# Attention by feature: sums over tokens turned, scores in row halves of the array, two heads gathered by DMA, and a new order of the first region

## The chip, the cores and the metric

One core of a Trainium2 chip. Its engines run side by side, each through its own list of instructions in order: TensorE (PE; its weight loads are shown apart as PEld), VectorE (DVE), ScalarE (ACT), GpSimd (POOL) and SyncE (SP), on whose queue all DMAs of this kernel are issued. The metric is the device time in microseconds (us), median of several runs; lower is better.

## What is computed

A gated linear attention with complex decays (4 batches, 8 heads, 768 tokens, 48 features a head), then a soft mixture of experts over all 3072 tokens, then a mixture with one expert a token. Cut to what matters here, the attention:

```python
mag = np.sqrt(a_re * a_re + a_im * a_im)
scale = np.minimum(mag, 0.999) / (mag + 1e-06)
for t in range(S):
    new_re = ar * S_re - ai * S_im        # ar, ai: a_re * scale, a_im * scale at t, by feature d
    new_im = ar * S_im + ai * S_re
    S_re, S_im = (new_re + kv, new_im)    # kv[d, e] = k[t, d] * v[t, e]
    y[:, :, t] = np.einsum('bhd,bhde->bhe', q[:, :, t], S_re)
x = attn_out.transpose(0, 2, 1, 3).reshape(B * S, H * D)
x = _moe_ref(x=x, **moe_kwargs)           # softmax over tokens, 8 experts x 4 slots, 384 -> 1024 -> 384
return _moe2_ref(x=x, **moe2_kwargs)      # one expert a token
```

## The kernel before

The tokens are worked on in 24 units of 128 tokens: 4 batches of 6 chunks. The program has three regions, one after the other, each with its instructions declared to a small scheduler (`Sched`) and then issued in an order written out by hand (`ORDER`, one string a region): a list of 16-bit numbers, each 4 x the number of the instruction + the variant, which says on which of two engines an instruction with a choice runs. The first region holds attention and the running softmax over tokens and ends with the slot inputs `siT`; the second holds the slot experts; the third the one expert a token and the output. The change is in the first.

In the first region, `decl_A` takes the decays of a group of one or two units (768 columns: 2 units x 384 features) through logarithms and an arctangent. `decl_B` makes, for a unit, the sums over its tokens of log decays and of phases: a product of a triangle of ones (`tri`) with a [128 tokens x 384 features] tile, result by token (`cumsum`, line 422 on). For most units it runs as two products in a shorter float format, of a high part (line 432 or 433) and a low part (434 or 435). The last token's sum is carried into the first row of the next unit's tile (lines 453 and 464, one partition of 384 columns), so a unit's sums start from those of the unit before; the first unit of a batch gets a start value (448). Then come the exponentials (455, 457), k and q times these (458, 459), rounding of the phases (466, 467) and, for a group, sine and cosine (475, 476).

`decl_C` multiplies k and q by cosine and sine into `kqp` (493; two instructions of 768 columns a unit, on VectorE or GpSimd), by token. Sixteen transposes a unit (503) turn it into 112-row tiles `kT`, `qT` (cosine part in rows 0 to 47, sine part in 64 to 111), which are copied from PSUM (helper `copy`, line 386, on ScalarE or VectorE). Scores of a head are one product of 112 rows (513), masked by VectorE (519). The output of a pair of heads comes from masked scores times v (526) and state times q (530), two heads side by side in the column halves of the array; the products of k and v (538) go the same way and are added to the state (559). The output is copied (`yT`), turned (569) and copied again (`x`). `decl_M` makes the running softmax over tokens for four units at a time.

The weights of the experts come on the same queue: eight arrays `wr` (1.5 MB each) during the first region, five arrays `wl` (line 364 too) that take the place of tiles of the first region as these become free, and the last three arrays in six halves (765) in the place of the first ones. The slot experts' first layer is line 748, the second 777.

Of the kernel before, what the change touches and what calls it, by code (L numbers as in the profile page):

```python
# [1355 lines left out]
```

## Time and profile before

| | |
|---|---|
| time, median of 3 runs | 331.19 us (330.14 to 333.09) |
| span of the profiled execution | 333.4 us |
| TensorE busy, whole span | 292.8 us (88%) |
| VectorE busy | 271.5 us (81%) |
| ScalarE busy | 223.9 us (67%) |
| GpSimd busy | 102.0 us (31%) |
| DMA moved | 57.98 MB |

Busy time is a share of the whole span; the regions have different limits, so the section of rows further down gives it by stretch. A row of the groups by line reads: line, engine, operation, written tile <- read tiles, shapes, count | busy time in us, mean duration in ns | idle time of the engine just ahead of these, and what ended it. Line 386 is a helper, there the tile tells. A float32 product has two records in the trace.

### The profile page before, as it was taken

What the parts mean: (1) busy time and instruction counts of PE and PEld (TensorE: products, weight loads), DVE (VectorE), ACT (ScalarE), POOL (GpSimd) and SP (SyncE); (2) the same over time, 40 slices, a digit from 0 to 9 for tenths busy, and PEclk for the clock granted to TensorE, in tenths of its full rate; (3) what the DMA queues carried; (4) which work ended last, traced back from release to release, by engine and by line L of the source; (5) the groups of instructions that cost most, each with busy time, mean ns of one, the idle gap of its engine ahead of it and who ended that gap; (6) DMA issues with size and microseconds to landing.
All of it is one profiled execution on the core that took longest, in us unless ns stands there. A gap on an engine that the chain in (4) does not pass through costs nothing. (4 is left out here: it accounts for less than half of the span.)

```text
span 333.4 us, 7852 instructions
## 1 busy us (share of the span) xinstructions
PE 292.8 (88%) x3152; PEld 230.4 (69%) x3152; DVE 271.5 (81%) x520; ACT 223.9 (67%) x417; POOL 102.0 (31%) x66
## 2 busy tenths in 40 slices
PE   0998989899886999998898969998999999999990
PEld 0676776778655779776587857887888433689880
DVE  3799999999999999999999998998555832557750
ACT  4999788689767889887878893887342321434670
POOL 0023456344515357533273553434400000000000
PEclk9999999979999999999979989999999999965996
DMA  7976887486574234235212320325693495290492
GB/s 231 298 317 241 308 312 262 170 312 229 168 243 152 77 80 159 73 105 180 73 49 73 101 81 12 94 73 191 201 361 77 132 375 186 47 334 1 154 328 96
DMA packets 27709, 57.98 MB, mean 174 GB/s; under 512 B 1824, under 2 KB 17568, under 8 KB 27664
## 3 DMA queue, kind: packets, MB, share of 16 engines
q1 hardware_dynamic: 27664, 57.39, 51.3%
q8 instruction: 27, 0.44, 0.5%
q14 instruction: 18, 0.15, 0.1%
HBM read 52.66 MB, written 4.72 MB: 172 GB/s over the span
## 5 line engine op out<-in xcount | busy, mean ns | idle before, releaser
L493 POOL TENSOR_TENSOR kqp<-kqi,lt 128x768 f32<-128x768 f32 x31 | 63.9, 2069 | 68.2 <-ACT lt L475 17.9
L503 PE MATMUL bank<-cst,kqp 128*112 128x128 f32 x384 | 54.3, 278 | 3.1 <-DVE lt L467 1.8
L513 PE MATMUL bank<-qT,kT 112*128 112x128 f32 x384 | 54.8, 289 | 1.9 <-DVE qT L386 1.8
L513 PEld LDWEIGHTS bank<-qT,kT 112*128 112x128 f32 x384 | 48.8, 198 | 6.8 <-DVE qT L386 2.4
L503 PEld LDWEIGHTS bank<-cst,kqp 128*112 128x112 f32 x384 | 41.9, 134 | 11.4 <-issue 6.5
L526 PE MATMUL bank<-sc,v 128*48 128x128 f32 x384 | 37.0, 279 | 3.8 <-DVE sc L519 2.0
L684 ACT ACT_TABLE_LOAD x29 | 37.2, 1283 | 1.2 <-PEq L1339 0.8
L519 DVE TENSOR_TENSOR sc<-bank,cst 128x512 f32<-128x512 f32 x48 | 32.5, 685 | 3.4 <-PE bank L513 2.8
L530 PE MATMUL bank<-qT,St 112*48 112x128 f32 x320 | 31.3, 272 | 0.0
L406 POOL TENSOR_TENSOR lt<-reim,lt 128x768 f32<-128x768 f32 (+1 forms) x11 | 19.4, 1760 | 34.9 <-ACT lt L405 34.3
L435 POOL TENSOR_TENSOR hl<-lt,hl 128x384 fp32r<-128x384 f32 x15 | 17.6, 1176 | 34.9 <-ACT hl L433 31.7
L526 PEld LDWEIGHTS bank<-sc,v 128*48 128x48 f32 x384 | 19.9, 122 | 10.1 <-issue 2.8
L538 PEld LDWEIGHTS bank<-v,kqp 128*48 128x48 f32 x640 | 18.0, 129 | 9.1 <-issue 4.0
L538 PE MATMUL bank<-v,kqp 128*48 128x48 f32 x640 | 22.2, 217 | 1.8 <-DVE St L559 1.3
L433 ACT ACTIVATE hl<-lt 128x384 fp32r<-128x384 f32 x28 | 14.5, 520 | 12.9 <-DVE lt L453 9.3
L439 PE MATMUL bank<-hl,trir 128*128 128x384 f32 x34 | 14.9, 437 | 5.8 <-DVE kqi L458 3.0
L1008 POOL TENSOR_TENSOR Pm<-G,pos 128x128 fp32r<-128x128 f32 x1 | 0.6, 644 | 63.0 <-DVE G L1003 63.0
L493 DVE TENSOR_TENSOR kqp<-kqi,lt 128x768 f32<-128x768 f32 x17 | 19.0, 1125 | 0.7 <-PE bank L538 0.7
L386 ACT COPY kT<-bank 112x512 f32<-112x512 f32 x28 | 16.3, 584 | 4.8 <-PE bank L503 4.8
L530 PEld LDWEIGHTS bank<-qT,St 112*48 112x48 f32 x320 | 19.3, 123 | 0.0
L682 PE MATMUL bank<-cst 128*48 128x128 f32 x78 | 11.0, 301 | 8.0 <-DMA cst<-cst 8.0
L386 DVE COPY qT<-bank 112x512 f32<-112x512 f32 x23 | 15.6, 683 | 2.4 <-PE bank L503 2.2
(248 smaller groups left out, 651.8 us busy)
## 6 DMA issues: line engine op xcount, KB each, us to landing
wr<-w SPq DMA_DIRECT2D x8, 1536.0 KB, 8.8
kqi<-kq SPq DMA_DIRECT2D x24, 384.0 KB, 3.4
reim<-reim SPq DMA_DIRECT2D x11, 768.0 KB, 5.5
wl<-w SPq DMA_DIRECT2D x5, 1536.0 KB, 7.2
v<-v SPq DMA_DIRECT2D x24, 192.0 KB, 2.4
wr<-w SPq DMA_DIRECT2D x6, 768.0 KB, 9.1
out<-osb SPq DMA_DIRECT2D x10, 384.0 KB, 2.6
wl<-m2w SPq DMA_DIRECT2D x2, 768.0 KB, 5.2
```

The costliest lines, as they stand in the source:

```text
L386: v = {"A": ("ACT", t_act(n, True), lambda: nc.scalar.copy(out=out, in_=in_()), False), "D": ("DVE", t_dve(n), lambda: vec.tensor_copy(out ...
L406: either("P", n, lambda e: e.tensor_tensor(out=l1, in0=im, in1=l0, op=ALU.mult), r=[kim] + k0, w=k1)
L435: e.tensor_tensor(out=hl[:, 1], in0=src, in1=hl[:, 0].bitcast(F32), op=ALU.subtract))
L439: pe.matmul(o(), trir, hl[:, 0], start=True, stop=False)
L493: either(e, 768, lambda e, dst=dst, j=j: e.tensor_tensor(out=dst, in0=kq, in1=b(j), op=ALU.mult), r=src + [kj], w=[kd])
L503: pe.transpose(bank(kb)[:112, 128 * i:128 * i + 128], o[:, j, 4 * hf + i], idn)
L513: pe.matmul(bank(kb)[:, 128 * i:128 * i + 128], kTt[ik[hf]][:, i], qTt[iq[hf]][:, i], start=True, stop=True)
L519: op("DVE", t_dve(512), lambda: vec.tensor_tensor(out=sct[ic[hf]], in0=b4(), in1=msk, op=ALU.mult), r=[kb], w=[ksc])
L526: pe.matmul(yps[64 * i:64 * i + 48, pr], v[:, 48 * h:48 * h + 48], sct[ic[hf]][:, h - 4 * hf], start=True, stop=(c == 0))
L530: pe.matmul(yps[64 * i:64 * i + 48, pr], St[:, h], qTt[iq[hf]][:, h - 4 * hf], start=False, stop=True)
L538: pe.matmul(kvps[64 * i:64 * i + 48, h, :48], o[:, 0, h, 64 * i:64 * i + 48], v[:, 48 * h:48 * h + 48], start=True, stop=True)
L684: tab = lambda t: nc.scalar.preload_act_table_set(TABLES[t])
```

## The change

All in the first region, with what hangs on it:

- k, q and the decays lie **by feature**: the host packs a unit's 384 features as three groups of 128, each with two heads of 48 in rows 0 to 47 and 64 to 111; heads 6 and 7 are cut in pieces of 16 rows that lie in rows 48 to 63 and 112 to 127 of the three groups (`feature_rows`).
- The sums over tokens are **turned**: the tile of decays is the stationary side, the triangle the moving one, three products of 128 columns, and the result is by feature. All are float32; high and low parts are gone, and so is the carry: sums start anew in each chunk. Phases get the last column of the unit before added (`pct`), and the state is multiplied by the chunk's whole decay (`Dt`) after each chunk.
- Products with cosine and sine go into `F` (by feature, so no turning is needed for the scores). The pieces of heads 6 and 7 are **gathered** from `F` into `M` by six DMAs a unit, 16 rows each.
- k alone is turned, for the products with v (six transposes in 20 units). Scores are products of 48 rows, cosine part and sine part added up, two heads at a time in the **row halves** of the array, each into a bank of its own. Products with the state use quarters of the array.
- Numbers of buffers change (k, q: 3 to 2), the first region has seven banks to pick from and one for k times v (before six, and one each for k times v and y), the scheduler knows the array's shapes (`MODE`), and the first region's order is a new string; so where DMAs, weights too, stand in SP's list is new.

By the new string, of 24 or 48 each: products F: 35 on VectorE, 13 on GpSimd; remainders of phases (20): 5 and 15; state products (20, four of them on VectorE only): 6 and 14; copies of turned k, 288 columns (40): 34 ScalarE, 6 VectorE; 96 columns (40): 29 and 11; copies of yT (48): 39 and 9; of x: 18 and 6; small copies of one or three columns: 27 ScalarE, 26 VectorE, 31 GpSimd. The arrays of `wr` go out in the order 3, 2, 0, 7, 5, 4, 6, 1; the array 4 ahead of the last unit's gathers, 6 and 1 after them, at the end of the list.

```diff
+XC = (0, 1, 0, 1)
+def pair(q):
+    return (2 * q + XC[q], 2 * q + 1 - XC[q])
+def feature_rows():
+    f = np.zeros((3, 128), np.int64)
+    for j in range(3):
+        for i in range(2):
+            f[j, 64 * i:64 * i + 48] = 48 * pair(j)[i] + np.arange(48)
+            f[j, 64 * i + 48:64 * i + 64] = 48 * pair(3)[i] + 16 * j + np.arange(16)
+    return f.reshape(-1)
-NR, NL, NK, NV, NKQ, NY, NX, NT, NTK, NTQ, NWR = 2, 3, 3, 4, 2, 4, 4, 2, 2, 3, 8
+NR, NL, NK, NV, NF, NKT, NSC, NY, NX, NWR = 2, 3, 2, 4, 2, 2, 4, 5, 5, 8
...
+MODE = [[0 if i == j else 95 if j else 24 for j in range(5)] for i in range(5)]
...
+            if e == "PE":
+                t0 = max(t0, free.get(e, 0.0) + MODE[mode][self.modes[i]])
...
@@ decl_B @@
+            def f():
+                for i in range(3):
+                    pe.matmul(bank(kb)[:, 128 * i:128 * i + 128], lt[:, j, 128 * i:128 * i + 128], (tri, tri2)[j], start=True, stop=True)
+            op("PE", 655, f, r=[kin, "cst"], w=[kb], acq=kb)
...
-            op("DVE", t_dve(384), lambda: vec.tensor_tensor(out=ln1, in0=oL()[96:97], in1=ln1, op=ALU.add), r=[kL, kn1], w=[kn1])
...
+        copy("D", 3, Dt[:, u, :3], lambda: oL3()[:, :, 127], r=[kL], w=[("D", u, 0)])
+        if c < NC - 1:
+            either("P", 3, lambda e: e.tensor_copy(out=Ft[u % NF][:, :, 512:513], in_=Dt[:, u, :3, None]), r=[("D", u, 0)], w=[("F", u % NF, 2)])
...
+            op("DVE", t_dve(384), lambda: vec.tensor_tensor(out=l3[1], in0=oP3(), in1=pct[(u - 1) % 2][:, :, None].to_broadcast([128, 3, 128]), op=ALU.add), r=[kP, ("pc", (u - 1) % 2)], w=[kth])
+            op("DVE", t_dve(384, True), lambda: vec.tensor_scalar(out=n, in0=lt[:, 1], scalar1=MAGIC, scalar2=MAGIC, op0=ALU.add, op1=ALU.subtract), two=True, r=[kth], w=[kn])
+            either("P", 384, lambda e: e.tensor_tensor(out=lt[:, 1], in0=lt[:, 1], in1=n, op=ALU.subtract), r=[kth, kn], w=[kth])
+        if c < NC - 1:
+            last = l3[1][:, :, 127]
+            op("DVE", 70, lambda: vec.tensor_copy(out=pct[u % 2], in_=last), r=[kth], w=[("pc", u % 2)], alt=(("ACT", 96, lambda: nc.scalar.copy(out=pct[u % 2], in_=last), False),))
@@ decl_C @@
-        Tr(0, 0, "A")
...
+        for i, e in ((0, "P"), (1, "D")):
+            b = lt[:, i].rearrange("p (j t) -> p j t", j=3)[:, None].to_broadcast([128, 2, 3, 128])
+            either(e, 768, lambda e, i=i, b=b: e.tensor_tensor(out=Fv[:, i], in0=kq, in1=b, op=ALU.mult), r=[(kkq, 0), (kkq, 1), klt(u, i)], w=[kF[i]])
+        for i in range(2):
+            for j in range(3):
+                d, o = 64 * i + 16 * j, 64 * i + 48
+                dma(32768, lambda j=j, d=d, o=o: nc.sync.dma_start(out=M[d:d + 16, :nx], in_=F[o:o + 16, j, :nx]), r=kF + kX, w=[("M", u % NF, i, j)])
+        if kX:
+            either("P", 1, lambda e: e.tensor_copy(out=Dt[:112, u, 3:], in_=M[:112, 512:513]), r=kM, w=[("D", u, 1)])
+        def kind(q, i, x):
+            t = F[64 * i:64 * i + 48, q] if q < 3 else M[64 * i:64 * i + 48]
+            return t[:, 128 * x:128 * x + 128]
...
+                        pe.transpose(bank(kb)[:, 128 * j:128 * j + 128], F[:, j, 128 * x:128 * x + 128], idn)
...
+                copy("A", 288, kTt[b][:, :288].rearrange("p (j i r) -> p j i r", j=3, i=2), lambda kv4=kv4: kv4()[:, :, :, :48], r=[kb], w=[("kT", b, 0)])
+                copy("D", 96, kTt[b][:, 288:].rearrange("p (i j r) -> p j i r", j=3, i=2), lambda kv4=kv4: kv4()[:, :, :, 48:], r=[kb], w=[("kT", b, 1)])
...
+                for q in qs:
+                    for x in range(2):
+                        for i in range(2):
+                            pe.matmul(bank(kbs[i])[:, 128 * q:128 * q + 128], kind(q, i, x), kind(q, i, 2 + x), start=(x == 0), stop=(x == 1))
...
+        op("PE", 870, SC((0, 1)), r=kF, w=kbs, acq=kbs[1], mode=2)
+        op("PE", 870, SC((2, 3)), r=kF + kM, w=kbs, mode=2)
...
+        def out(q, i, m):
+            o = 64 * (i ^ XC[q])
+            return bank(kby[XC[q]])[o:o + m, 128 * (q // 2):128 * (q // 2) + 128]
...
+                        pe.matmul(out(q, i, 64), v[:, 48 * h:48 * h + 64], sct[scs[i]][:, q], start=True, stop=(c == 0))
...
+                for x in range(2):
+                    for q in qs:
                         for i in range(2):
+                            pe.matmul(out(q, i, 48), S[64 * i:64 * i + 48, q, 48 * x:48 * x + 48], kind(q, i, 2 + x), start=False, stop=(x == 1))
...
+                op("DVE", t_dve(384), lambda: vec.tensor_tensor(out=Ut, in0=kvv, in1=S, op=ALU.add), r=[("kv", 0), ("kv", 1), kS], w=["U"])
+                either("P", 384, lambda e: e.tensor_tensor(out=S1, in0=Ut, in1=dcy, op=ALU.mult), r=["U"] + kD, w=[kS1])
...
+            copy("A", 256, yT[:, i::2], lambda i=i: bank(kby[i])[:112, :256].rearrange("p (q t) -> p q t", q=2), r=[kby[i]], w=[(kyT, i)])
...
-    s.emit(tab, fill(6), 600, 400, kv_last[0], kv_first[0], WARM)
+    s.emit(tab, fill(7), 600, 400, kv_last[0], kv_first[0], WARM)
```

## Rows read from the trace of the kernel before

**Rows 1.** The page: its first line.

```profile
span 333.4 us, 7852 instructions
```

**Rows 2.** The chain of waits, around and behind the end of the first region: start, length, what.

```profile
260.90 0.25 ACT siT L386
...
279.62 5.30 PE bank L777 x64
```

**Rows 3.** Busy time by stretch: stretch, length, each engine, granted clock, DMA share, GB/s.

```profile
0.00:20.00 20.00, 11.62 (x54) 7.98 (x54) 12.07 (x23) 14.56 (x22) 2.02 (x9) 1.00 0.88 290
20.00:200.00 180.00, 160.16 (x1874) 130.67 (x1874) 176.37 (x306) 150.50 (x269) 82.69 (x48) 0.98 0.50 166
200.00:236.00 36.00, 33.60 (x414) 28.53 (x414) 31.58 (x60) 24.56 (x50) 14.16 (x8) 0.98 0.28 87
236.00:261.20 25.20, 24.55 (x318) 20.56 (x315) 15.48 (x37) 8.89 (x24) 2.46 (x1) 1.00 0.76 249
```

**Rows 4.** Groups of instructions by line, VectorE.

```profile
L453 DVE TENSOR_TENSOR lt<-bank,lt 1x384 f32<-1x384 f32 x20 | 11.2, 558 | 1.0 <-ACT bank L455 0.5
...
L434 DVE SCALAR_TENSOR_TENSOR hl<-lt,hl 128x384 fp32r<-128x384 f32 x18 | 13.8, 769 | 0.0
...
L432 DVE TENSOR_SCALAR hl<-lt 128x384 fp32r<-128x384 f32 x6 | 2.1, 353 | 0.0
...
L386 DVE COPY qT<-bank 112x512 f32<-112x512 f32 x23 | 15.6, 683 | 2.4 <-PE bank L503 2.2
...
L493 DVE TENSOR_TENSOR kqp<-kqi,lt 128x768 f32<-128x768 f32 x17 | 19.0, 1125 | 0.7 <-PE bank L538 0.7
...
L466 DVE TENSOR_SCALAR n<-bank 128x384 bf16<-128x384 f32 x24 | 13.1, 551 | 0.2
```

**Rows 5.** Groups of instructions by line, ScalarE.

```profile
L386 ACT COPY kT<-bank 112x512 f32<-112x512 f32 x28 | 16.3, 584 | 4.8 <-PE bank L503 4.8
...
L433 ACT ACTIVATE hl<-lt 128x384 fp32r<-128x384 f32 x28 | 14.5, 520 | 12.9 <-DVE lt L453 9.3 <-DVE lt L464 3.6
...
L386 ACT COPY x<-bank 128x384 f32<-128x384 f32 x13 | 6.2, 475 | 0.8 <-PE bank L569 0.7
```

**Rows 6.** Groups of instructions by line, GpSimd.

```profile
L493 POOL TENSOR_TENSOR kqp<-kqi,lt 128x768 f32<-128x768 f32 x31 | 63.9, 2069 | 68.2 <-ACT lt L475 17.9 <-ACT lt L476 14.6 <-PE bank L538 9.5
...
L435 POOL TENSOR_TENSOR hl<-lt,hl 128x384 fp32r<-128x384 f32 x15 | 17.6, 1176 | 34.9 <-ACT hl L433 31.7 <-PE bank L616 3.2
```

**Rows 7.** Products: the chain of waits, then the timeline (start, length, engine, line).

```profile
238.29 0.88 PE bank L503 x8
...
239.52 0.22 PE bank L530 x4
...
241.64 0.89 PE bank L513 x8
...
229.68 0.45 PE L439 MATMUL bank<-hl,trir 128*128 128x384 f32 x1
...
229.97 0.34 PE L440 MATMUL bank<-hl,trir 128*128 128x384 f32 x1
```

**Rows 8.** DMA issues (count, KB each, median us to landing); the queue of SP.

```profile
v<-v SPq DMA_DIRECT2D x24, 192.0 KB, 2.4
...
wr<-w SPq DMA_DIRECT2D x8, 1536.0 KB, 8.8
...
3.13 2.15 SPq L423 DMA_DIRECT2D v<-v  x4
```

**Rows 9.** The queue of SP, the last product kqp, and stretches with weights under way.

```profile
224.96 30.29 SPq L364 DMA_DIRECT2D wl<-w  x5
...
237.46 2.46 POOL L493 TENSOR_TENSOR kqp<-kqi,lt 128x768 f32<-128x768 f32 x1 [2.97 <-ACT qT L386]
...
236.00:248.00 12.00, 12.00 (x173) 10.16 (x173) 6.87 (x10) 3.35 (x6) 2.46 (x1) 1.00 0.97 324
...
271.00:279.00 8.00, 8.00 (x89) 2.83 (x81) 3.29 (x9) 0.00 (x0) 0.00 (x0) 1.00 1.06 371
```

More of the change, by code (lines that the diff above doesn't have):

```diff
@@ L141, in place @@
         fb = [(0.0, b) for b in range(self.nbanks)]
-        order, end, port, cur, held = [], 0.0, 0.0, self.tab, {}
+        order, end, port, cur, held, mode = [], 0.0, 0.0, self.tab, {}, 0
         heap = [(key[i], i) for i in range(n) if nd[i] == 0]
@@ L250, in put @@
         c[:, o:o + w] = a
-    tri = (PERM[:, None] <= PERM[None, :]).astype(np.float32)
+    tri = np.triu(np.ones((128, 128), np.float32))
     put("tri", tri)
@@ L419, in decl_B @@
         lt = lt_of(u)
+        l3 = [lt[:, j].rearrange("p (j t) -> p j t", j=3) for j in range(2)]
         kln, kth = klt(u, 0), klt(u, 1)
@@ L508, in SC @@
-        def SC(hf):
-            kb = s.bank()
-            def f():
-                for i in range(4):
-                    pe.matmul(bank(kb)[:, 128 * i:128 * i + 128], kTt[ik[hf]][:, i], qTt[iq[hf]][:, i], start=True, stop=True)
-            op("PE", 870, f, r=[("kT", ik[hf]), ("qT", iq[hf])], w=[kb, ("sc", ic[hf])], acq=kb)
-            msk = tri[:, None].to_broadcast([128, 4, 128])
-            b4 = lambda: bank(kb).rearrange("p (h t) -> p h t", h=4)
-            ksc = ("sc", ic[hf])
-            op("DVE", t_dve(512), lambda: vec.tensor_tensor(out=sct[ic[hf]], in0=b4(), in1=msk, op=ALU.mult), r=[kb], w=[ksc])
@@ new lines, in decl_C, with SC @@
+        kbs = [s.bank() for _ in range(2)]
+        scs = [(2 * u + i) % NSC for i in range(2)]
+        def SC(qs):
+            def f():
+                for q in qs:
+                    for x in range(2):
+                        for i in range(2):
+                            pe.matmul(bank(kbs[i])[:, 128 * q:128 * q + 128], kind(q, i, x), kind(q, i, 2 + x), start=(x == 0), stop=(x == 1))
+            return f
+        op("PE", 2, lambda: None, r=kF, w=[kbs[0]], acq=kbs[0], mode=2)
+        op("PE", 870, SC((0, 1)), r=kF, w=kbs, acq=kbs[1], mode=2)
@@ new lines, in decl_C, with f @@
+        op("PE", 870, SC((2, 3)), r=kF + kM, w=kbs, mode=2)
+        for i in range(2):
+            msk = tri[:, None].to_broadcast([128, 4, 128])
+            op("DVE", t_dve(512), lambda i=i, msk=msk: vec.tensor_tensor(out=sct[scs[i]], in0=bank(kbs[i]).rearrange("p (h t) -> p h t", h=4), in1=msk, op=ALU.mult), r=[kbs[i]], w=[("sc", scs[i])])
+        if c < NC - 1:
+            for x in range(2):
+                t, kt = kTs[x]
+                def f(x=x, t=t):
+                    for q in range(4):
+                        for i in range(2):
+                            w = t[:, 96 * q + 48 * i:96 * q + 48 * i + 48]
+                            h = pair(q)[i]
+                            pe.matmul(kvps[64 * i:64 * i + 48, q, 48 * x:48 * x + 48], w, v[:, 48 * h:48 * h + 48], start=True, stop=True)
+                kv_first.append(len(s.ops))
+                op("PE", 472, f, r=kt + [kv] + ([("kv", 0)] if x else []), w=[("kv", x)], mode=1)
@@ new lines, in decl_C, with intra @@
+        kby = [s.bank() for _ in range(2)]
+        kS = ("S", (u - 1) % 2)
+        S = St[(u - 1) % 2]
+        def out(q, i, m):
+            o = 64 * (i ^ XC[q])
+            return bank(kby[XC[q]])[o:o + m, 128 * (q // 2):128 * (q // 2) + 128]
+        def intra(qs):
+            def f():
+                for q in qs:
+                    for i in range(2):
+                        h = pair(q)[i]
+                        pe.matmul(out(q, i, 64), v[:, 48 * h:48 * h + 64], sct[scs[i]][:, q], start=True, stop=(c == 0))
+            return f
@@ L562, in decl_C @@
         yT, kyT = yTt[u % NY], ("yT", u % NY)
-        copy("A", 512, yT, lambda: yps[:112], r=[("y", 0), ("y", 1)], w=[kyT])
+        for i in range(2):
+            copy("A", 256, yT[:, i::2], lambda i=i: bank(kby[i])[:112, :256].rearrange("p (q t) -> p q t", q=2), r=[kby[i]], w=[(kyT, i)])
         kb = s.bank()
@@ L1167, in build @@
             nc.sync.dma_start(out=p96, in_=a["phi96"])
[L1168 removed]
             def load_x(u):
                 b0, t0 = ORD[u][0] * 4 * D, ORD[u][1] * 128
[L1172 to L1174 removed]
+                for i in range(2):
+                    nc.sync.dma_start(out=xu[:, :, i], in_=ysc[t0:t0 + 128, i, b0:b0 + 4 * D].rearrange("t (q e) -> t q e", e=D))
             for u in range(NU):
@@ L1316, in layout @@
     return {
-        "reim": pack("a_re", "a_im"),
-        "kq": pack("k", "q"),
+        "reim": np.ascontiguousarray(pack("a_re", "a_im")[..., rows]),
+        "kq": by_feature("k", "q"),
         "v": pack("v").reshape(NU, 128, DM),
@@ L1353, in unpack @@
     for u, (b, c) in enumerate(ORD):
-        out[b, c, PERM] = o[u]
+        out[b, c] = o[u]
     return out.reshape(B * S, DM)
```

278 lines of the change are left out of this document (120 added, 158 removed).

## The prediction

> **What bounds the kernel now.** I read the busy time by stretch first, then the chain of waits at the end, then the groups of instructions by line. All sums are made on the profiled execution, whose span is 333.4 us [rows 1]; the median of the three timed runs is 331.19, so the last step takes 2.2 us off. The first region (attention and the running softmax over tokens) ends when siT is written, at 261.2; the rest takes 72.2 us [rows 1, 2]. In the long middle of that region, 20 to 200 us, VectorE works 176.4 of 180 us, 98%; TensorE has 160 there, ScalarE 150, GpSimd 83 [rows 3]. So what ends last in the middle is the queue of VectorE. Only in the last 25 us before siT is TensorE the fuller one, 24.55 of 25.2 (97%), with VectorE at 15.5 [rows 3]. Over the first region VectorE sums to 12.1 + 176.4 + 31.6 + 15.5 = 235.5 us, TensorE to 229.9, ScalarE to 198.5, GpSimd to 101.3 [rows 3].
>
> **The change part by part.** The order table is a list of numbers, each 4 x instruction + variant. Read against the declarations it says which engine takes each instruction, and in which order; for the kernel before these counts are those of the trace (18 low parts and 17 products kqp on VectorE, 28 high parts on ScalarE) [rows 4, 5], so I use them for the new one.
>
> *VectorE, removed.* The carries from one unit into the first row of the next: 20 + 20 at 0.558 us though they touch one partition, 22.3. Low parts 18 x 0.769 and high parts 6 x 0.353: 16.0. Copies of turned k and q: 43 x 0.683 = 29.4. State sums and copies, 17 at 0.55: 9.3. Products kqp: 17 x 1.125 = 19.1. Rounding and remainder of the phases, 48 x 0.55: 26.4. Copies of yT (9 x 0.683) and x (11 x 0.55): 12.2. Together 134.7 [rows 4].
>
> *VectorE, added.* Products F, 35 of 48 here: 35 x 1.125 = 39.4. Phases: 20 sums and 8 first-chunk steps at 0.55, 20 roundings from SBUF at 0.353 (the rate of the high parts), 5 remainders at 0.55: 25.2. The rows for 384 columns (0.55) and 512 (0.683) give about 0.15 us + 1.04 ns a column. By that the copies of turned k, 6 of 288 and 11 of 96, are 5.5, and 9 of yT with 256 and 6 of x 7.1. State: 16 sums and 6 products at 0.55, 12.0. 26 copies of one or three columns at 0.15: 3.9. Three more products l1 here at 1.1: 3.3. Together 96.4 [rows 4]. Net -38: about 197.
>
> *ScalarE.* Removed: 53 turned copies at 0.585, 28 high parts at 0.520, 15 copies of yT, 13 of x and 3 of the state: 62. Added, by the same two-point rule (384 columns 0.475, 512 columns 0.584): 34 copies of 288 at 0.39, 29 of 96 at 0.23, 39 of 256 at 0.37, 18 of x, 27 small ones at some 0.2: 48. Net -14: 184 at most [rows 5]. *GpSimd.* 31 products of 2.07 become 13; 15 low parts of 1.18 become 15 remainders and 14 state products of that size: from 101 to about 82 [rows 6].
>
> *TensorE.* Eight transposes take 0.88 us, 0.11 each: 16 a unit become 6 in 20 units and none in 4, so 41.9 become 13.1. A float32 product of 128 columns is 0.22 (four, as eight records, 0.89). A sum over tokens is now three of these, 0.66, 48 times: 31.7. Before, 34 split pairs (the second product starts 0.29 after the first, so 0.58 a pair) and 14 whole ones of 384 columns, 0.66, made 29.0 [rows 7]. So +3. The scores: 8 products a unit with 112 rows become 16 with 48 rows, two at a time in two row halves of the array. No row of the trace shows row halves. The nearest is the column halves: two such products, four records, take 0.22, the time of one [rows 7]. From below, 0.22 a pair gives 8 x 24 x 0.22 = 42 for the region, as before; from above, 0.44 gives 84. I take 0.22, the row it is nearest to: in both, the two products share no part of the array and, with a bank for each half, no place of the result. The Trainium skill, "TensorEngine Tiling (Array Packing)", sections "Theoretical Speedup" and "Gotcha 1: PSUM Pressure", says that a contraction of at most 64 rows can run up to twice as fast, and that two row halves must not write one bank at once; no run here shows it yet. The products with the state, 8 a unit in column pairs, become 16 in quarters, four at a time: 0.22 for four is 18, as now; as pairs 35. The others stay. The array changes its shape 142 times by the new order, 148 by the old. Net -26: 229.9 become about 204.
>
> *Chains.* The sums no longer wait for the unit before. The phases keep a chain (sum, round, remainder, a copy of three columns, next unit), about 2.5 us a unit against some 9 for a unit, so hidden. The state gets a product, 1.2 us on GpSimd [rows 6], between two units, behind the next unit's scores.
>
> *The gathers.* Six DMAs a unit, 33 KB each, 144 in all, on the one queue of SP among loads of 192 KB to 1.5 MB. SP issues four v in 2.15 us, and a v of 192 KB has landed after 2.4 [rows 8]; so a full M comes about 6 x 0.54 + 2.4 = 5.6 us after F. From below they cost nothing, as the first scores and other units' sums, transposes and state products stand ahead of the scores that read M; from above each waits behind a weight (8.8 to landing [rows 8]). With a unit every 9 to 10 us I count them hidden. If that cover is gone, all of TensorE's later products stand behind the waiting one, and the masks and copies behind these; on SP the next kq (two buffers now) stands behind gathers that wait for F.
>
> *The weights.* Before, the five arrays wl go out from 225.0 on, after all of wr [rows 9]. In the new SP order the arrays 6 and 1 of wr stand behind the last unit's gathers. The last product kqp ends at 239.9, 21 us before siT [rows 9]; the new tail holds the same products, so they go out some 19 us before siT. From there 2 arrays, 5 arrays and 6 halves must pass, 15.7 MB: 42.4 us at 371 GB/s [rows 9] and about 2 to land, so until 25 after siT. The last products that need them start 21.1 after siT now (32 of the 64 records from 279.62, after half of 5.3) [rows 2]. So the experts wait about 4 us. At 324 GB/s [rows 9] it is 10; if the tail stretches, 0.
>
> **The sum.** TensorE becomes the fullest (204, against 197 and 184). It is busy 229.9 of 261.2 us now, 88%, and 97% in the last 25, where VectorE has room. I keep 88%: three engines then lie within 10% of each other, and a wait of one shows. 204 / 0.88 = 232 for the first region, 29 less. With 4 behind it: 333.4 - 29 + 4 = 308.4, less 2.2: 306. At 93% (219) it is 293; at 84% (243) with 8 of waiting 321. This, 293 to 321, is the likeliest case's own range.
>
> **Rivals.**
> *Row halves take turns.* The scores cost 42 more and the state products 18: TensorE 264. At 97% the region is 272, with no wait for weights behind it: 333.4 + 11 - 2 = 342; at 90% 363. Against it: column halves run side by side [rows 7]. It decides the sign, at 88%, from 26 of those 60 us, 0.32 a pair. Chance 0.10.
> *The gathers lie on the way.* For: one queue, in order, 8.8 us behind a weight [rows 8], and in the new SP order a weight or a load of reim stands just ahead of the gathers of some ten units. Against: between 20 and 200 the DMA engines are half empty (0.50) [rows 3]. 1.2 us a unit uncovered takes the 29 back: 335; half of that is 320. Chance 0.15, mostly 318 to 340. If their fixed times did not overlap, six at 2.4 are 14.4 us a unit, 346 for the region and over 410 in all; four v issued in 2.15 us [rows 8] speak against it, and I leave it 0.02 of the 0.15. The Trainium skill, "DMA: Bandwidth & Descriptors", section "Bandwidth", has the rule to batch to 1 MiB and calls transfers under 64 KB descriptor-dominated: it speaks against gathers of 33 KB.
> *TensorE closes up.* With less on VectorE it could be as dense as in the last 25 us, 97%: 210 + 72 + 4 - 2 = 284. For: that stretch [rows 3]. Against: masks and copies still stand between its products. Chance 0.13.
> *Nothing moves*, because the region hangs on ScalarE's or on pure latency. VectorE's 98% speaks against it [rows 3]. 331; chance 0.04.
>
> **How the numbers follow.** Forecast 0.58, rivals 0.10, 0.15, 0.13, 0.04. A difference under 1% is about what a measurement of this kernel can't tell from none. Faster by more, under 328: 0.58 + 0.13 + 0.08 of the gathers = 0.79. Within 1%: 0.04 + 0.05 = 0.09. Slower, over 334.5: 0.10 + 0.02 = 0.12. The range goes from 285 (it takes in over half of TensorE closing up) to 328 (half of the gathers); some 0.2 is left out, mostly above.
>
> **What would show it.** VectorE under 92% in the middle, without one-partition sums; eight score products of 48 rows in 0.88 us, or in 1.75; TensorE's idle ahead of the second half of the scores, put down to a DMA of M or not; siT near 232; products of w2 waiting for wl. I am wrong if siT comes before 215 or after 250, or if the experts wait over 10 us.

## The result, and the profile after

The changed kernel takes 320.19 us (median of six runs, 317.35 to 324.12); the kernel before, beside it, 331.21 (329.54 to 333.09). The ratio is 0.965, with a 95% interval from 0.959 to 0.971. Forecast were 306: the time lies in the range of 285 to 328, but the gain is 11 us where 25 were forecast. The profiled execution took 322.03 us, with a span of 320.0 where the kernel before had 333.4 [rows 1]. In every execution that has both, the time stands 1.7 to 2.2 us above the span, so by estimate the profiled one of the kernel before took some 335 us, longer than any of the six timed; compared by span, the change looks some 2 us better than by medians.

The first region ended nearly where it was expected, the rest did not. Here is the chain of waits of the changed kernel from the last unit on (start, length, what). L505 are the products F, L509 the gathers, L543 the scores, L797 and L826 the two layers of the slot experts (L748 and L777 before), L837 the step behind them.

```profile
216.62 1.82 DVE F L505 x2
...
221.62 3.11 DMA M<-F
...
224.86 0.81 PE bank L543 x7
...
235.35 0.27 DVE siT L411
...
235.67 6.56 PE bank L797 x48
...
256.92 11.79 DMA wr<-w
268.75 4.47 PE bank L826 x28
273.22 1.54 PE bank L837 x12
```

siT is written at 235.6 instead of 261.2 [rows 2]: 25.5 us earlier. But the experts' second layer ends at 273.22, 37.6 us after siT, where it took 23.7 before [rows 2]; and the chain there is no longer TensorE's but a transfer of weights, which lands at 268.7. The queue of SP and the stretches say the same (stretch, length, PE, PEld, DVE, ACT, POOL, granted clock, DMA share, GB/s):

```profile
218.50 3.71 SPq L509 DMA_DIRECT2D M<-F  x6
222.25 2.10 SPq L389 DMA_DIRECT2D wr<-w  x2
224.45 19.51 SPq L389 DMA_DIRECT2D wl<-w  x5
244.05 14.83 SPq L814 DMA_DIRECT2D wr<-w  x6
```

```profile
0.00:20.00 20.00, 11.69 (x79) 10.43 (x79) 10.61 (x21) 14.32 (x20) 1.63 (x13) 1.00 0.65 237
20.00:200.00 180.00, 165.75 (x2656) 140.93 (x2656) 159.25 (x300) 147.98 (x309) 74.89 (x75) 0.97 0.55 168
200.00:215.00 15.00, 13.36 (x255) 11.63 (x254) 11.37 (x23) 8.12 (x19) 1.19 (x2) 1.00 0.51 165
215.00:235.70 20.70, 18.87 (x296) 14.41 (x290) 11.61 (x38) 6.21 (x23) 1.78 (x3) 0.98 0.72 274
235.70:265.40 29.70, 25.44 (x209) 8.23 (x210) 10.71 (x19) 4.55 (x10) 0.00 (x0) 0.90 1.06 373
```

In the middle VectorE has gone from 176.4 to 159.3 of 180 us and TensorE from 160.2 to 165.8 [rows 3]. Behind siT the DMA engines are full at 373 GB/s. The two arrays of wr that stand behind the last unit's gathers go out at 222.25, and all that stands behind them is late with them.

These groups answer to those of before (busy us, mean ns, then idle time ahead of them and what ended it):

```profile
L505 DVE TENSOR_TENSOR F<-kqi,lt 128x768 f32<-128x768 f32 x35 | 39.7, 1158 | 3.7 <-PE bank L590 2.7 <-issue 0.4 <-ACT lt L490 0.3
...
L470 DVE COPY F<-Dt 128x3 f32<-128x3 f32 x6 | 2.6, 430 | 0.0
...
L609 POOL TENSOR_TENSOR St<-Ut,Dt 112x384 f32<-112x384 f32 x14 | 13.0, 929 | 19.1 <-DVE Ut L607 19.0
...
L543 PE MATMUL bank<-M 48*128 48x128 f32 x192 | 18.8, 284 | 8.6 <-DMA M<-F 7.2 <-issue 1.2
```

The gathers are not quite hidden: TensorE waits 7.2 us for M in seven places, 0.3 us a unit.

### The profile page after: what moved, and what is told of

The parts are those of the page before. It is cut to its first block, busy times and chain, and to the rows that moved or that the text cites. A ratio compares the mean times of both kernels' runs of the same rounds, so it can differ in the third digit from the quotient of the medians.

```text
span 320.0 us, 9381 instructions
## 1 busy us (share of the span) xinstructions
PE 278.9 (87%) x3764; PEld 220.0 (69%) x3764; DVE 230.3 (72%) x478; ACT 202.1 (63%) x423; POOL 80.1 (25%) x94
## 4 chain that ended last, share of the span: by engine, by line
PE 46%; DVE 11%; DMA 9%; SPq 9%; issue 3%; ACT 1%; DVEq 0%; ACTq 0%
PE bank L543 6%; PE bank L581 5%; PE bank L457 5%; SPq L509 5%; DMA M<-F 5%; PE bank L590 4%; DMA wr<-w 4%; SPq L814 3%; DVE F L505 3%; PE bank L797 3%; PE bank L563 3%; PE bank L528 2%; PE bank L618 2%; PE bank L1121 1%; PE bank L826 1%
## 5 line engine op out<-in xcount | busy, mean ns | idle before, releaser
L457 PE MATMUL bank<-cst,lt 128*128 128x128 f32 x288 | 41.3, 287 | 9.4 <-DMA cst<-cst 8.3
L457 PEld LDWEIGHTS bank<-cst,lt 128*128 128x128 f32 x288 | 36.4, 197 | 11.8 <-ACT lt L435 8.3
L505 DVE TENSOR_TENSOR F<-kqi,lt 128x768 f32<-128x768 f32 x35 | 39.7, 1158 | 3.7 <-PE bank L590 2.7
L543 PE MATMUL bank<-F 48*128 48x128 f32 x576 | 41.1, 284 | 0.4 <-DVE kqi L466 0.3
L543 PEld LDWEIGHTS bank<-F 48*128 48x128 f32 x576 | 36.4, 192 | 5.0 <-issue 1.6
L552 DVE TENSOR_TENSOR sc<-bank,cst 128x512 f32<-128x512 f32 x48 | 31.3, 684 | 10.4 <-PE bank L543 9.9
L581 PE MATMUL bank<-sc,v 128*64 128x128 f32 x384 | 31.9, 292 | 2.6 <-DMA v<-v 1.8
L505 POOL TENSOR_TENSOR F<-kqi,lt 128x768 f32<-128x768 f32 x13 | 24.9, 1925 | 29.2 <-PE bank L590 14.5
L581 PEld LDWEIGHTS bank<-sc,v 128*64 128x64 f32 x384 | 21.6, 143 | 8.1 <-issue 4.5
L543 PE MATMUL bank<-M 48*128 48x128 f32 x192 | 18.8, 284 | 8.6 <-DMA M<-F 7.2
L590 PE MATMUL bank<-F,St 48*48 48x128 f32 x480 | 25.6, 283 | 0.0
L528 PE MATMUL bank<-cst,F 128*128 128x128 f32 x120 | 20.1, 286 | 3.9 <-DVE F L505 2.9
L543 PEld LDWEIGHTS bank<-M 48*128 48x128 f32 x192 | 15.3, 188 | 10.8 <-issue 7.4
L826 PE MATMUL bank<-wl,hT 128*32 128x384 f32 x80 | 16.0, 601 | 4.3 <-DMA wl<-w 4.3
## 6 DMA issues: line engine op xcount, KB each, us to landing
wl<-w SPq DMA_DIRECT2D x5, 1536.0 KB, 17.2
```

The lines of the kernel that those rows point to most:

```text
L457: pe.matmul(bank(kb)[:, 128 * i:128 * i + 128], lt[:, j, 128 * i:128 * i + 128], (tri, tri2)[j], start=True, stop=True)
L505: either(e, 768, lambda e, i=i, b=b: e.tensor_tensor(out=Fv[:, i], in0=kq, in1=b, op=ALU.mult), r=[(kkq, 0), (kkq, 1), klt(u, i)], w=[kF[i]])
L528: pe.transpose(bank(kb)[:, 128 * j:128 * j + 128], F[:, j, 128 * x:128 * x + 128], idn)
L543: pe.matmul(bank(kbs[i])[:, 128 * q:128 * q + 128], kind(q, i, x), kind(q, i, 2 + x), start=(x == 0), stop=(x == 1))
L552: op("DVE", t_dve(512), lambda i=i, msk=msk: vec.tensor_tensor(out=sct[scs[i]], in0=bank(kbs[i]).rearrange("p (h t) -> p h t", h=4), in1=m ...
L581: pe.matmul(out(q, i, 64), v[:, 48 * h:48 * h + 64], sct[scs[i]][:, q], start=True, stop=(c == 0))
```

## The experiments

Theory: the weights that go out late cost the tail its 12 us, and the first region behaves about as forecast. Rivals: the missing gain lies in the first region, in the gathers, or in row halves that run in turn; or it is a loss of clock. This table is worked out from the profile of each run: where TensorE takes siT up, its busy and idle time up to there, the granted clock up to there (an average over the levels of 1.2 and 2.4 GHz; full is 1.00), the time at the lower level that this clock stands for (added up in steps of 1 us), the experts (from there to the step behind their second layer), and the rest. Each row is one execution.

| kernel | siT | PE busy | PE idle | clock | lower level | experts | rest |
|---|---|---|---|---|---|---|---|
| before | 261.2 | 229.9 | 31.3 | 0.98 | 10 | 23.7 | 48.5 |
| changed | 235.7 | 209.7 | 26.0 | 0.98 | 11 | 37.6 | 46.8 |
| after_again | 237.2 | 211.1 | 26.1 | 0.96 | 17 | 36.0 | 46.8 |
| weights_early | 243.2 | 215.1 | 28.1 | 0.95 | 24 | 25.6 | 45.7 |
| one_more_late | 242.1 | 215.0 | 27.1 | 0.95 | 24 | 40.4 | 43.1 |
| weights_early_same_banks | 242.3 | 214.2 | 28.1 | 0.95 | 24 | 24.3 | 43.1 |
| covered | 238.8 | 212.8 | 26.0 | 0.97 | 14 | 29.0 | 46.1 |
| no_gather_read | 230.8 | 207.0 | 23.8 | 0.97 | 14 | 38.0 | 42.1 |
| halves_in_turn | 241.5 | 222.8 | 18.7 | 0.97 | 15 | 35.8 | 46.3 |
| one_half | 288.9 | 275.6 | 13.3 | 0.87 | 75 | 33.8 | 47.3 |
| scores_twice | 239.4 | 224.1 | 15.3 | 0.99 | 3 | 35.9 | 47.0 |
| mask_twice | 243.3 | 212.9 | 30.4 | 0.97 | 14 | 36.5 | 47.1 |

The clock has to be kept in mind when two rows are compared. Here the same eight records, in the last unit of the changed kernel and of weights_early_same_banks, at the higher and the lower level:

```profile
227.51 0.59 PE bank L581 x8
```

```profile
231.80 1.05 PE bank L582 x8
```

So 1.05 us at the lower level do the work of 0.59, and by this a microsecond there costs TensorE some 0.44 (an estimate; less where it would have waited anyway).

**The late weights.** `weights_early` moves two transfers in the list of SyncE: w6 behind unit 11's v, w1 behind group 3's re and im (the planner then picked other PSUM banks from unit 1 on).

```diff
+        for i, j in moves:
+            x = seq[seq // 4 == i]
+            seq = seq[seq // 4 != i]
+            seq = np.insert(seq, int(np.flatnonzero(seq // 4 == j)[0]) + 1, x)
...
-    s.follow(ORDER[0])
+    s.follow(ORDER[0], ((1361, 636), (1356, 187)))
```

> The changed kernel, with the two arrays of wr that stand at the end of SP's list (6 and 1) moved ahead: one behind the fourth load of reim, one behind v of unit 11, both at places where SP stood idle for 4 us or more. Theory A, the tail of weights is the missing part: 3.15 MB less behind the last gathers, at 373 GB/s 8.4 us, and with less idle the array keeps its clock in the second layer; the experts (siT to the last product of the second layer, 37.5 us now, 23.7 before the change) take 26 to 29, the first region stays within 2 us of 235.7, the whole is 308 to 312. Theory B, the experts are slow for another reason (the array's clock, the order of the products): they stay at 35 to 38 and the whole at 318 to 322. Theory C, weights between the gathers hold these up: the experts get short, but the first region grows by 5 to 10 and the whole stays at 316 to 322.

316.01 us (314.01 to 316.57), ratio to before 0.950 (0.944 to 0.956). The experts take 25.6 us instead of 37.6. The queue of SP and the chain show where the 12 us went:

```profile
228.21 12.15 SPq L393 DMA_DIRECT2D wl<-w  x5
```

```profile
254.02 11.99 DMA wr<-w
266.05 2.77 PE bank L830 x28
```

From the first weight behind the last gathers to the last landing it is 37.8 us for 46.5: 8.7 us are the two arrays, for which 8.4 were expected. 1.6 come from a longer cover (15.0 us from there to siT, for 13.4), and 1.7 from the last 28 records, 2.77 us at the higher clock level for 4.47. But siT came 7.5 us later. `one_more_late` does the opposite: w5 too goes out at the end of the list, behind w1.

```diff
-    s.follow(ORDER[0])
+    s.follow(ORDER[0], ((1360, 1356),))
```

> The changed kernel with one array more (5) moved to the very end of SP's list, behind 6 and 1: 1.57 MB more in the tail, 4.2 us at 373 GB/s. Theory A: the experts take 41 to 42.5 us after siT (37.5 now), the first region the same or 0 to 2 us less. Theory B: 37 to 38.

327.49 us, experts 40.4, just below the 41 to 42.5 of theory A: 2.8 to 4.4 us more than in the two profiles of the changed kernel. The last weights land 37.6 us after siT for 33.1 and 33.2 there, 4.4 to 4.5 more, and one array at 373 GB/s takes 4.2. Here too siT came late, 242.1, though no transfer had been moved into the first region. So I took the changed kernel's profile once more:

> The changed kernel as it is, profiled once more beside the other runs of this call. Its first profile wrote siT 235.4 us after the span began, while two edits that should not have touched the first region wrote it at 241 to 243. Theory A (a run of the first region differs from the next by several us, so single profiles of it compare only to some 6 us): siT anywhere from 232 to 243, the time 317 to 324. Theory B (the first region repeats to about 1 us, and the later siT of those two edits is theirs): siT 234.5 to 236.5. In both the slot experts take 37 to 38 us from siT to the end of their second layer.

322.19 us, siT at 237.2, experts 36.0: between the two theories. Two profiles differ by 1.5 us, but that is no bound: the six timed executions of the changed kernel have spans of 315.3 to 322.0, at mean clocks of 0.956 to 0.931. The experts are 1.6 us shorter because the last records ran at the higher level here, after the same wait:

```profile
270.47 2.77 PE bank L826 x28
```

And the early weights with nothing else touched, banks included:

```diff
-        for t0, i, t in sorted(order, key=lambda x: x[0]):
+        at = {i: t0 for t0, i, _ in order}; order = [(at[m[i]] + .01 if i in m else t0, i, t) for t0, i, t in order]
+        for t0, i, t in sorted(order, key=lambda x: x[0]):
...
-    s.emit(tab, fill(7), 600, 400, kv_last[0], kv_first[0], WARM)
+    s.emit(tab, fill(7), 600, 400, kv_last[0], kv_first[0], WARM, ((1361, 636), (1356, 187)))
```

> As weights_early (w6's transfer right behind unit 11's v, w1's right behind group 3's re and im in the list of SyncE), but all else of the first region stays as it was, the banks of PSUM too: weights_early had other banks in the products and copies from unit 1 on, and its siT came 7.4 us later than the changed kernel's. Theory A (the late weights cost the tail some 12 us and the moved transfers cost the first region nothing; the 7 us were of the banks or of the run): siT as in the changed kernel run beside it within 2 us, the slot experts in 25 to 26 us, the time 307 to 311. Theory B (weights that cross the first region's transfers hold up its v, kq and gathers): siT 5 to 8 us later than in the changed kernel run beside it, the time 314 to 317.

Its profiled execution is the fastest of all runs, 311.50; the other three took 317.03 to 320.62, so the median is 317.76 and the ratio 0.968 (0.956 to 0.980), too spread to say how large the gain is. The experts again run as before, on TensorE alone (chain of waits):

```profile
242.26 5.36 PE bank L798 x48
...
260.69 5.83 PE bank L827 x64
266.52 1.54 PE bank L838 x12
```

The tail is as theory A has it, siT (242.3) as theory B has it. Here are the changed kernel, its second profile and this one, up to siT:

```profile
0.00:235.70 235.70, 209.66 (x3268) 177.40 (x3270) 192.83 (x379) 176.63 (x369) 79.49 (x93) 0.98 0.57 183
```

```profile
0.00:237.20 237.20, 211.14 (x3264) 178.91 (x3264) 193.06 (x379) 176.71 (x369) 80.89 (x93) 0.96 0.57 181
```

```profile
0.00:242.30 242.30, 214.17 (x3268) 180.78 (x3270) 192.91 (x379) 177.14 (x369) 80.87 (x93) 0.95 0.61 196
```

The same products cost TensorE 3 to 4.5 us more at a lower granted clock, and its idle time is 2 us longer. At most those 2 us can be waits for moved transfers. The time at the lower level is 24 us, for 11 and 17 in the changed kernel; at 0.44 these 7 to 13 us are 3 to 6 of the 5 to 6.6 by which siT is late. Most of it lies at the very end: from the first scores that read the last M to siT it takes 15.1 us (227.2 to 242.3), for 10.8 (224.9 to 235.7) in the changed kernel, and from 230 to 235 the clock is 0.50. `one_more_late` has 24 us of the lower level too, with no transfer moved into the first region. So siT came as late as theory B has it, but at most 2 us of that by its mechanism; whether the early weights have a part in the clock stays open.

**Row halves.** `one_half` has all scores read rows 0 to 47, so the heads of the second half get other scores and no two neighbours lie in different row halves:

```diff
-    pe.matmul(bank(kbs[i])[:, 128 * q:128 * q + 128], kind(q, i, x), kind(q, i, 2 + x), start=(x == 0), stop=(x == 1))
+    pe.matmul(bank(kbs[i])[:, 128 * q:128 * q + 128], kind(q, 0, x), kind(q, 0, 2 + x), start=(x == 0), stop=(x == 1))
```

> The scores of all eight heads read rows 0 to 47 alone (heads in the second half get the scores of the first half's heads: another computation, the same number and shapes of products). Theory A (two products in the two row halves run side by side, a pair in 0.25 us where one takes 0.22): without it 16 products take 16 times 0.22, 3.5 us a unit for 1.99, TensorE's busy time in the first region rises by 24 times 1.53, some 37 us, and siT comes 33 to 40 us later than in the changed kernel run beside it. Theory B (row halves give nothing by themselves; a product of 48 rows is as quick alone): 2.0 to 2.2 us a unit and siT within 3 us.

371.8 us. The timeline of TensorE, two units in a row, after_again first, then one_half, both at a granted clock of 1.00:

```profile
107.17 1.61 PE L543 MATMUL bank<-F 48*128 48x128 f32 x24 [0.29 <-DVE kqi L466]
108.62 0.61 PE L543 MATMUL bank<-M 48*128 48x128 f32 x8
109.06 1.51 PE L543 MATMUL bank<-F 48*128 48x128 f32 x24
```

```profile
80.07 2.94 PE L543 MATMUL bank<-F 48*128 48x128 f32 x24
82.86 1.05 PE L543 MATMUL bank<-M 48*128 48x128 f32 x8
83.75 1.95 PE L543 MATMUL bank<-F 48*128 48x128 f32 x16
```

From one unit's start to the next it is 1.89 us with row halves and 3.68 without: 0.24 a pair, against 0.23 for each product alone. The halves run side by side. 24 times 1.79 is 43 us; siT came 52 to 53 later, the rest at a clock of 0.87 (75 us at the lower level). The Trainium skill, "TensorEngine Tiling (Array Packing)", section "Theoretical Speedup", gives up to twice the speed for at most 64 rows; the trace agrees, 3.68 to 1.89 is 1.95.

`halves_in_turn` keeps the products but issues four of one half, then four of the other:

```diff
-    for q in qs:
-        for x in range(2):
-            for i in range(2):
+    for i in range(2):
+        for q in qs:
+            for x in range(2):
```

> The changed kernel with the loops of the scores exchanged: all products of the first row half of the array, then all of the second, so that neighbours never lie in different halves; same products, same banks. If neighbours in different halves run side by side, as the rows give (16 products in 1.99 us, 0.25 a pair), each pair now costs twice as much: 8 x 24 x 0.22 to 0.25 = 42 to 48 us more on TensorE, the first region 33 to 48 longer and the whole 345 to 365. If they do not, and the 0.25 a pair has another reason, nothing moves: 318 to 323.

325.53 us. TensorE's busy time rises by 12 to 13 us, for 42 to 48 expected, where none of the pairs are neighbours but at the borders of fours. So the pairing survives in part; how, no row shows.

**The gathers.** `no_gather_read` has the scores and state products of the last two heads read F in place of M (other values, the same shapes); the gathers still run.

```diff
-    t = F[64 * i:64 * i + 48, q] if q < 3 else M[64 * i:64 * i + 48]
+    t = F[64 * i:64 * i + 48, q % 3]
```

> The changed kernel, but scores and state products of heads 6 and 7 read the rows of heads 0 and 1 in F in place of the gathered M, so these outputs are another computation; the gathers are still issued and only the decay lane waits for them. If the gathers are hidden but for the 7 us that the trace puts down to them, the first region ends 4 to 9 us earlier (227 to 232). If they set the pace of the region, as a whole queue of products stands behind each, it ends 15 us or more earlier. Behind siT the weights come no earlier than the last gathers, so a part of any gain is given back there.

312.64 us; siT 4.9 and 6.4 us ahead of the two profiles of the changed kernel, 2.2 of them from less idle time on TensorE, the rest from shorter busy time, for which no row gives the reason. The time at the lower level, 14 us, lies between those of the two profiles, so the clock doesn't explain it. Reading M thus costs some 5 us, by one execution. `covered` tries to hide it: on top of the early weights the products that read M go out one to three steps later in eleven units.

```diff
-    s.emit(tab, fill(7), 600, 400, kv_last[0], kv_first[0], WARM, ((1361, 636), (1356, 187)))
+    s.emit(tab, fill(7), 600, 400, kv_last[0], kv_first[0], WARM, ((1361, 636), (1356, 187), (576, 608), (609, 471), (673, 848), (716, 685), (787, 790), (894, 694), (941, 910), (1005, 1033), (1105, 1151), (1226, 1258), (1259, 1229)))
```

> weights_early_same_banks, and on TensorE alone the score products of the last two heads (the ones that read the gathered M) go out one to three steps later in eleven of the 24 units (9 to 13, 15 to 17, 19, 21, 22), behind another unit's first score products or behind cumulative, state or logit products that need no gather. Theory A (TensorE's waits for the gathers, 7 to 8 us in the first region, are lost time that other products can cover): these waits fall to 4 us or less, siT comes 3 to 5 us earlier than in weights_early_same_banks at the same granted clock, and the time is 311 to 315. Theory B (the masks behind the later scores come later by as much, and VectorE or the next products wait for them instead): the waits fall, but siT and the time stay within 2 us of weights_early_same_banks, 315 to 319.

314.91 us (313.03 to 316.68), ratio 0.953 (0.944 to 0.962). The waits of TensorE for M (us in total, times, longest), first with the early weights alone, then covered:

```profile
PE bank L544 <- DMA M<-F: 7.8, 9, 1.9
```

```profile
PE bank L544 <- DMA M<-F: 5.9, 6, 1.9
```

They fall by 2 us where some 4 were expected, and siT comes 3.5 us earlier. But the lower level has 14 us here for 24, and at 0.44 these 10 us are 4.5: the clock alone explains it. The time is in theory A's range and no better than that of weights_early (316.01; the intervals overlap), so that covering the waits gains anything is not shown. The experts take 29.0 here: with siT at 238.8 the last weights, landing at 263.3, are late again.

**Which engine sets the first region.** `scores_twice` issues half of the scores twice, `mask_twice` one mask of two twice; both compute the same.

```diff
-        op("PE", 870, SC((0, 1)), r=kF, w=kbs, acq=kbs[1], mode=2)
+        op("PE", 870, SC((0, 1, 0, 1)), r=kF, w=kbs, acq=kbs[1], mode=2)
```

> The eight score products of the first two heads of each half are issued twice in each unit (same result): 24 times 0.995 us, 23.9 us more of TensorE, nothing else changed. Theory A (TensorE, busy 89% of the first region, sets its length): siT 21 to 25 us later than in the changed kernel run beside it, TensorE's share at 89 to 91%. Theory B (VectorE, 88% busy in the middle, sets it as much, or the chain of one unit through the engines does): TensorE fills its idle time first; 25 us of it are idle, siT comes 5 to 14 us later and its share rises to 94% or more.

324.51 us, siT at 239.4, 2.2 to 3.7 us later. But this execution had only 3 us of the lower level, for 11 and 17; at 0.44 that is worth 3.5 to 6 us, so at an equal clock it would be some 7 to 8 later. That is theory B's range; theory A is out either way.

```diff
-    op("DVE", t_dve(512), lambda i=i, msk=msk: vec.tensor_tensor(out=sct[scs[i]], in0=bank(kbs[i]).rearrange("p (h t) -> p h t", h=4), in1=msk, op=ALU.mult), r=[kbs[i]], w=[("sc", scs[i])])
+    op("DVE", t_dve(512), lambda i=i, msk=msk: [vec.tensor_tensor(out=sct[scs[i]], in0=bank(kbs[i]).rearrange("p (h t) -> p h t", h=4), in1=msk, op=ALU.mult) for _ in range(2 - i)], r=[kbs[i]], w=[("sc", scs[i])])
```

> The mask of the first half's scores is applied twice in each unit (same result): 24 times 0.684 us, 16.4 us more of VectorE, nothing else changed. Doubling half of the scores (23.9 us more of TensorE by its price) moved siT by only 2 to 4 us, so TensorE alone does not set the first region. Theory A (VectorE, busy 193 of 236 us and 88% in the middle, sets it as much): siT 10 to 16 us later than the 235 to 237 us of the changed kernel. Theory B (neither engine alone sets it: each has some 25 to 43 us of idle time that further work fills first): siT at 236 to 241 us and VectorE's busy time 16 us higher.

328.93 us, siT at 243.3, 6.1 to 7.6 us later, with a time at the lower level (14 us) between those of the two profiles: between the theories. `one_more_late` came about as late with no work added, so one execution gives this price to a few us only. Busy times up to siT, scores_twice first:

```profile
0.00:239.40 239.40, 224.13 (x3648) 194.74 (x3648) 188.90 (x379) 177.15 (x369) 78.86 (x93) 0.99 0.56 180
```

```profile
0.00:243.30 243.30, 212.92 (x3268) 179.33 (x3269) 207.63 (x403) 177.61 (x369) 81.00 (x93) 0.97 0.56 177
```

In scores_twice TensorE's idle time shrank from 26.0 to 15.3, and its waits for M from 7.2 to 2.4: it took up most of the added work in time that it had stood idle. In mask_twice VectorE's shrank from 43 to 36. Neither engine alone sets the region. (By its price the work added on TensorE is some 23 us, 96 pairs at 0.24, and its busy time rose by 13 to 14.5; the higher clock explains 3.5 to 6 of the difference, the rest stays open. On VectorE 14.8 us more of busy time cost 6 to 8.)

## Why the prediction was wrong

**The step that failed** is the weights' term: "So the experts wait about 4 us." They took 13.8 us longer; 12.0 of it is the wait for the last weights, which landed 33.1 us after siT where the products had needed them 21.1 after it. That the landing hangs on when the weights go out, four runs show: from the first weight behind the last gathers to the last landing it is 46.0 to 46.5 us in the changed kernel's two profiles and in no_gather_read, and 37.8 in weights_early with two arrays less. The mechanism was the one described, and the text names "if the experts wait over 10 us" as what would make it wrong; the size was off in three places.
- "They go out some 19 us before siT": it was 13.4 (222.25 to 235.67). I took the stretch from the last product kqp to siT, 21 us [rows 9], over from the old tail. In the new one the scores don't stand behind eight transposes and their copies: the last F ends at 218.4, 17.2 before siT, and the six gathers ahead of the weights hold SP for 3.7 us. The tail that the change shortens was the cover of the weights behind it. That is 5.6 us, and the step that went wrong most.
- The ten arrays' worth of data took 46.5 us to the last landing, for 44.4 forecast (42.4 at the 371 GB/s of [rows 9] and 2 to land): 2 us. The rate behind siT was as taken, 373; over the whole 46.5 us it was 340.
- The last 28 records ran in 4.47 us, against 2.65 for 32 of them before (half of the 5.30 in [rows 2]): 2 us. The granted clock was 0.62 in these 4.47 us. I had no term for the clock, and this part belongs to the one execution: in after_again the same records took 2.77 after the same wait. The 4 us that were forecast and these 9.7 make the 13.8.

**The first region** was right to 4 us: 25.5 earlier (24 in the second profile) for 29. Its parts: VectorE 192.8 us for 197, ScalarE 176.6 for "184 at most", GpSimd 79.5 for 82, TensorE 209.7 for 204. TensorE's missing 5.7 are in part the pairs of scores, 0.24 to 0.25 where 0.22 was taken, 192 times: 4 to 6 us. Its share, 89%, is the 88% that I kept. But the reason given was weaker than the number: "TensorE becomes the fullest" is so, yet it doesn't set the region alone, as scores_twice shows.

**The rivals.** Row halves in turn: no, side by side. Gathers on the way: a small part was there, some 5 us, where the rival needed 1.2 us a unit to take the gain back; it was 0.2 to 0.3. The Trainium skill, "DMA: Bandwidth & Descriptors", section "Bandwidth", calls transfers under 64 KB descriptor-dominated; here one of 32 KB lands after 2.1 to 2.4 us (medians), and most of that is covered. TensorE closing up to 97%: no; even with work added it came to 94% in scores_twice and 95% in one_half. Nothing moves: no.

**The chances.** Faster by over 1% was right. The range came from the first region's cases and kept the tail's term at 4 to 8 us in all of them. With 13.4 us in place of 19 the term is 9.6 and the sum 314 for a forecast span of 308.4; to the measured 320.0 it lacks 3.7 us in the first region and some 4 in the stream and the last products, less 1.7 that the rest of the tail gave (46.8 for 48.5). The 2.2 us taken off at the end fit only the one execution of the kernel before: the changed kernel's median lies 0.2 above its span. So by medians the miss is 14 us and not 11.6.

**Where the gain can be had.** The early weights, with or without covered gathers, give ratios of 0.950 and 0.953 to before (0.968 in weights_early_same_banks): medians 2.4 to 5.3 us below the changed kernel, not 12. In the profiles the tail gives back 8 to 17 us and the first region takes 1.6 to 7.5, which goes mostly with the granted clock.

## What to carry to other kernels

When a region gets shorter, ask what its end covered: transfers with a fixed amount of data behind it do not get shorter with it, and what no longer fits under its end is waited for, unless it is issued earlier. Measure the cover on the new order's own tail (here from the last F to siT, with the issue time of the gathers ahead in the queue), not on the old one. And where two engines lie within 10% of each other, no one of them prices a change: at an equal clock, 23 us of work added on the fullest cost some 7 to 8, and 15 on the second fullest 6 to 8, by one execution each. Before such single executions are compared, add up their time at the lower clock level: here it differed by up to 13 us between runs of the same products.

## What the runs showed of the hardware

The granted clock falls without idling ahead of it. In one_half TensorE is busy at least 98% of the time in all three of these stretches; in the first the clock is 1.00, in the other two it is on average 0.74, between its levels of 1.2 and 2.4 GHz:

```profile
80.00:100.00 20.00, 20.00 (x259) 17.83 (x258) 15.90 (x34) 15.74 (x34) 7.65 (x9) 1.00 0.42 127
100.00:120.00 20.00, 19.75 (x215) 17.97 (x213) 11.49 (x19) 11.14 (x19) 4.12 (x7) 0.74 0.45 137
120.00:140.00 20.00, 19.68 (x204) 17.22 (x206) 13.43 (x27) 11.52 (x23) 8.32 (x7) 0.74 0.32 102
```

scores_twice, with 94% busy, had 0.99 over the region. The Trainium skill, "TensorE: Matmul & The Clock Gate", section "Part 1: The HAM clock gate", has the gate open with activity and close with idleness; these rows are not explained by that, and why the clock falls in them stays open.

A mean can hide one long wait. The six copies of three columns on VectorE (L470) have a mean of 0.43 us, where the estimate was 0.15; but five of them took 0.16, and one 1.78. That one lies beside a product F on GpSimd and ends with it, at 122.3:

```profile
119.74 2.53 POOL L505 TENSOR_TENSOR F<-kqi,lt 128x768 f32<-128x768 f32 x1 [3.12 <-DVE reim L436]
```

```profile
120.51 1.78 DVE L470 COPY F<-Dt 128x3 f32<-128x3 f32 x1
```

On GpSimd the 14 copies have a mean of 0.47, a median of 0.19 and a longest of 0.93.
